# Top-k attention and gated FFN on one core: TensorE's order stated from step 14, six weight splits inside it, an even pace for the first FFN unit, and another row order in odd batches

## The chip, the cores and the metric

The kernel runs on one core of one Trainium2 chip. The metric is the device time of one execution in microseconds (us). Before the change three runs gave 1627.73, 1629.19 and 1631.22 us, median 1629.19. The core has five engines that run side by side and meet through semaphores: TensorE (PE; its weight load is listed apart as PEld), VectorE (DVE), ScalarE (ACT), GpSimd (POOL) and SyncE (SP). In this kernel SP issues every DMA, from one queue in program order.

## The reference

Eight batches of eight heads, 576 rows, head dimension 64. Each row of the scores keeps its 32 largest entries; the result of the attention, 4608 x 512, goes through a gated FFN:

```
scores = scale * np.matmul(q, k.transpose(0, 1, 3, 2))
kth = np.partition(scores, -top_k, axis=-1)[..., -top_k:-top_k + 1]      # top_k = 32
scores = np.where(scores >= kth, scores, -1000000000.0)
scores = scores - np.max(scores, axis=-1, keepdims=True)
attn = np.exp(scores)
attn = attn / (np.sum(attn, axis=-1, keepdims=True) + 1e-09)
x = np.matmul(attn, v)            # then 4608 rows x 512
gate = 1.0 / (1.0 + np.exp(-(x @ w_gate)))      # 512 x 1536
val = x @ w_val                                 # 512 x 1536
return gate * val @ w_out                       # 1536 x 512
```

The weights are handed over as 64-bit floats.

## The kernel before

**Attention.** Heads go in pairs (NP = 4 pairs). A batch's 576 rows are four tiles of 128 rows (i = 0 to 3) and a tile of the 64 remaining rows (i = 4). One step is one tile of one pair: 20 steps a batch, 160 in all. A batch is worked in two groups of tiles (`halves`, line 58), and a group goes through all four pairs before the next begins. In loop turn n, `begin(n+2)` multiplies the scores of step n+2 (`pss`), `choose(n)` starts the selection of step n (DVE's MAX8 rows, ACT's exponentials, POOL's products `u`) and ends that of step n-1, `turned(n-2)` transposes (`pt`), and `weighed` multiplies a group's attention with the values (`po`). Its result `xf` is split into a leading part `xh` (ACT, L371) and a rest `xl` (POOL, L372), both fp32r.

**FFN.** The 4608 rows go in 12 units of U = 384 rows. A unit is a generator of 432 matmuls; it is pulled forward piece by piece by `more(goal)`, between the attention's own chunks. Each product is three matmuls, of leading and rest parts (L404 to L406 for the two first products, L428 to L430 for the last). A unit uses 18 weight tiles of 1 MB: 12 for gate and value (indices 0 to 11) and 6 for the output (12 to 17), in the order 0 1 2 3, 12 13 with 4 drawn ahead of them from unit one on, 5 6 7, 14 15, 8 to 11, 16 17.

**Weights.** `split_weight` (L124) turns a 64-bit weight tile into a leading and a rest part, in two halves: a load of raw bits (`wraw`, L136), ACT L143, L147, L151, DVE L144 to L146, POOL L149 (two multiplies), PE L152 to L154 into a PSUM tile `wrest`, ACT L155, and a store to a DRAM tile `ws` (L156). The first 12 are split in steps 0 to 11. The six last (8 to 11, 16, 17) are split by the first FFN unit's own `load` (L381 to L387), which keeps the split tile in SBUF and uses it there. Every other `load` fetches the tile from `ws` (L389). All of these tiles, split or loaded, come from one pool `w` of three buffers, in turn; a tile can be filled only when the buffer's former tile has had its last reader, and a split tile that isn't kept is read last by its store to `ws`.

**What sets the order.** SP, DVE, ACT and POOL run what a scheduler arranged, in a fixed order per engine. PE's order is the scheduler's, too, until the splits are over (`split_done`, L158, called at L539 after unit 0 has been run to its end); from there it is the order in which the program states it (`tc.manual_schedule`, L566). `goal` (L577) says how far the FFN should be: `at` counts the rows that attention has finished, the FFN follows 480 rows behind (`BEHIND`), but unit 0, once its 384 rows are there, at 1.5 times attention's pace:

```
goal = max(at - BEHIND, min((at - U) * 1.5, U)) * per_row
```

An engine runs its instructions in order: while one waits, all behind it wait as well. This holds for SP's DMAs.

Of the kernel before, what the change touches and what calls it, by code (L numbers as in the profile page):

```python
# [29 lines left out]
def tile_topk_attention_then_gated_ffn(  # L30
# [27 lines left out]
    halves = {0: ((0, 3), (3, NT + 1)), 1: ((0, 2), (2, NT + 1))}  # L58
    groups = [(b, *half) for b in range(B) for half in halves[b % 2]]
# [3 lines left out]
    BEHIND = 480  # L63

    LOADED, HELD = 12, 0
# [50 lines left out]
    ready, stored = {}, set()  # L116
# [7 lines left out]
    def split_weight(idx, held):  # L124

        wt = pools["w"].tile([P, 2, 2, NP, P], F32R, tag="w", name=f"wsplit_{idx}")  # L130
        if held:
            ready[idx] = wt
        for i in range(2):
            raw = pre_pools["raw"].tile([P, NP * P, 2], U32, tag="raw", name=f"wraw_{idx}_{i}")
            half = slice(i * NP * P, (i + 1) * NP * P)
            nc.sync.dma_start(raw.rearrange("p n t -> p (n t)"), w[idx][:, half].bitcast(U32))  # L136
            low, top = raw[:, :, 0], raw[:, :, 1]
            pair = wt[:, i].rearrange("p a c n -> p a (c n)")
            lead = pre_pools["parts"].tile([P, NP * P], F32, tag="lead", name=f"wt_lead_{idx}_{i}")
            rest = ps_f.tile([P, NP * P], F32, tag="f", name=f"wrest_{idx}_{i}")  # L140
# [234 lines left out]
    def ffn(nm0, xs, t0, general, early):  # L375
# [87 lines left out]
    def run(general):  # L463
        steps = [(g, p, i) for g, (_, first, end) in enumerate(groups) for p in range(NP) for i in range(first, end)]
# [3 lines left out]
        def fetch_keys(m):  # L468
            if m < len(steps) and steps[m][2] == groups[steps[m][0]][1]:
                g, p, _ = steps[m]  # L470
                b, first, _ = groups[g]
                if first == 0:
                    keys[b, p] = load_keys(b, p, f"{mark}{g}_{p}")

        def fetch_values(m):
            if m < len(steps) and steps[m][2] == groups[steps[m][0]][1]:
# [29 lines left out]

        def more(upto):
# [8 lines left out]
        def turned(m):  # L516
            g, p, i = steps[m]
            b, first, end = groups[g]
            if i == first:
# [3 lines left out]
            ets[g, p].append((et, P if i < NT else REM))  # L523
            yield from turn(e, inv, i, et, f"{mark}{b}_{i}_{p}")

        def weighed(m):
            nonlocal unit
            g, p, i = steps[m]
            b, first, end = groups[g]
            if i < end - 1 or (g, p) not in ets:  # L530
                return
            t, left, pieces = b * S + first * P, sum(n for _, n in ets[g, p]), []
# [12 lines left out]
            if p == NP - 1:  # L545
                while (unit + 1) * U <= b * S + min(end * P, S):
                    todo.append(ffn(f"{mark}{unit}", [xs[unit, d] for d in range(NP)], unit * U, general, unit > 0))
# [13 lines left out]
        per_row = 3 * (2 * NF * NP + NE * NF)  # L561
        region = None

        for n in range(len(steps) + 3):
            if not general and region is None and len(bxs) == 2:
# [3 lines left out]
            if region is None and not general and n < len(steps) and steps[n][0] == 0:  # L569
                early, steps0 = LOADED + HELD, 3 * NP  # L570
                for t in range(n * early // steps0, (n + 1) * early // steps0):
                    split_weight(order[t], t >= LOADED)
                    stored.add(order[t])
            fetch_values(n)
            fetch_keys(n + KEYS)
            ask(n + ASK)
            goal = max(at - BEHIND, min((at - U) * 1.5, U)) * per_row  # L577
# [10 lines left out]
            else:  # L588
# [9 lines left out]
                for chunk in (first, second):  # L598
                    for _ in chunk:
                        pass  # L600
            if 2 <= n < len(steps) + 2:
                at += (P if steps[n - 2][2] < NT else REM) / NP
# [74 lines left out]
```

## Time and profile before

| | us |
|---|---|
| runs: lowest, median, highest | 1627.73, 1629.19, 1631.22 |
| the profiled execution's own time | 1630.14 |
| its span in the trace | 1628.3 |
| PE busy in the span | 1546.7 (95%) |
| PEld, DVE | 1420.9 (87%), 1247.9 (77%) |
| ACT, POOL | 1166.1 (72%), 1176.5 (72%) |
| first FFN matmul starts | 180.02 |
| last FFN unit | 1546.4 to 1621.4 |

The span is the time from the trace's first to its last instruction; 1.8 us of the execution lie outside it. A busy time is the sum over an engine's instructions. "Idle before" is the time for which an engine stood still ahead of an instruction, put down to the releaser that came last. PEclk is the granted TensorE clock, as a share of 2.4 GHz. A row of a view of stretches ("windows") gives for each engine the busy time in the stretch and, after x, the number of instructions.

### The profile page before, as it was taken

What the parts mean: (1) busy time and instruction counts of PE and PEld (TensorE: products, weight loads), DVE (VectorE), ACT (ScalarE), POOL (GpSimd) and SP (SyncE); (2) the same over time, 40 slices, a digit from 0 to 9 for tenths busy, and PEclk for the clock granted to TensorE, in tenths of its full rate; (3) what the DMA queues carried; (4) which work ended last, traced back from release to release, by engine and by line L of the source; (5) the groups of instructions that cost most, each with busy time, mean ns of one, the idle gap of its engine ahead of it and who ended that gap; (6) DMA issues with size and microseconds to landing.
All of it is one profiled execution on the core that took longest, in us unless ns stands there. A gap on an engine that the chain in (4) does not pass through costs nothing.

```text
span 1628.3 us, 35823 instructions
## 1 busy us (share of the span) xinstructions
PE 1546.7 (95%) x11378; PEld 1420.9 (87%) x11378; DVE 1247.9 (77%) x5764; ACT 1166.1 (72%) x2551; POOL 1176.5 (72%) x1907
## 2 busy tenths in 40 slices
PE   5787999989999999999999999999999999999998
PEld 2344797779999999999999999999999999999998
DVE  5999768968888779878889679788888679877100
ACT  5988658967867678777768678777778678767322
POOL 3869858887876887787876887787786887765323
PEclk9989899999999999999999999999999999999999
DMA  7556754655555665565555665565555665564475
GB/s 221 179 174 193 283 202 142 218 183 200 201 199 190 222 217 193 195 240 185 216 187 197 214 233 188 201 221 204 194 204 180 212 223 195 185 214 157 175 286 183
DMA packets 89000, 330.05 MB, mean 203 GB/s; under 512 B 9952, under 2 KB 36576, under 8 KB 61920
## 3 DMA queue, kind: packets, MB, share of 16 engines
q1 hardware_dynamic: 88800, 327.65, 58.0%
q8 instruction: 92, 1.51, 0.4%
q14 instruction: 108, 0.88, 0.2%
HBM read 299.30 MB, written 28.31 MB: 201 GB/s over the span
## 4 chain that ended last, share of the span: by engine, by line
PE 68%; DVE 10%; POOL 5%; ACT 5%; issue 2%; DMA 1%; POOLq 0%; ACTq 0%; DVEq 0%
PE pz L404 11%; PE pz L405 10%; PE pz L406 10%; PE pss L225 8%; PE po L364 7%; PE pt L328 5%; PE po L428 5%; PE po L429 5%; PE po L430 5%; DVE cand L291 3%; DVE e L245 2%; DVE kths L317 2%; POOL u L309 2%; ACT under L303 1%; POOL k L177 1%
## 5 line engine op out<-in xcount | busy, mean ns | idle before, releaser
L309 POOL TENSOR_TENSOR u<-s,under 128x288 f32<-128x288 f32 x576 | 412.2, 738 | 71.7 <-ACT under L303 59.8
L404 PE MATMUL pz<-xh,w 128*128 128x384 f32 x1120 | 405.5, 362 | 2.0 <-ACT xh L371 2.0
L291 DVE MAX8 cand<-s 128x8 f32<-128x72 f32 x2304 | 343.5, 217 | 68.7 <-ACT s L233 56.0
L405 PE MATMUL pz<-xl,w 128*128 128x384 f32 x1120 | 378.0, 338 | 3.6 <-POOL xl L372 3.6
L406 PE MATMUL pz<-xh,w 128*128 128x384 f32 x1120 | 378.4, 338 | 0.0
L245 DVE SCALAR_TENSOR_TENSOR e<-s,kths,e 128x576 f32<-128x576 f32 x288 | 280.8, 986 | 30.7 <-ACT e L240 29.8
L303 ACT ACTIVATE under<-s,leads 128x576 fp8e4<-128x576 f32 x288 | 222.5, 774 | 91.3 <-DVE leads L295 75.3
L317 DVE MAX8 kths<-u 128x8 f32<-128x584 f32 x288 | 219.1, 761 | 63.1 <-POOL u L310 60.8
L240 ACT ACTIVATE e<-s,st 128x576 f32<-128x576 f32 x288 | 209.9, 773 | 43.3 <-PE pt L328 36.6
L416 POOL TENSOR_TENSOR gl<-gf,gh 128x384 fp32r<-128x384 f32 x144 | 153.6, 1067 | 107.3 <-ACT gh L415 104.6
L404 PEld LDWEIGHTS pz<-xh,w 128*128 128x128 f32 x1120 | 212.1, 189 | 8.7 <-issue 4.6
L405 PEld LDWEIGHTS pz<-xl,w 128*128 128x128 f32 x1120 | 212.7, 190 | 5.3 <-POOL xl L372 4.8
L334 ACT ACTIVATE et<-pt 128x384 f32<-128x384 f32 (+1 forms) x384 | 194.9, 521 | 28.4 <-PE pt L328 24.5
L406 PEld LDWEIGHTS pz<-xh,w 128*128 128x128 f32 x1120 | 211.5, 189 | 0.0
L328 PE MATMUL pt<-ident,e 128*128 128x128 f32 x1152 | 193.1, 277 | 11.0 <-DVE e L245 5.5
L428 PE MATMUL po<-gh,w 128*128 128x384 f32 x560 | 201.1, 360 | 0.0
L429 PE MATMUL po<-gl,w 128*128 128x384 f32 x560 | 188.9, 337 | 5.2 <-POOL gl L416 5.2
L430 PE MATMUL po<-gh,w 128*128 128x384 f32 x560 | 188.4, 336 | 0.0
L364 PEld LDWEIGHTS po<-et,v 128*64 128x64 f32 x1600 | 160.2, 138 | 30.6 <-issue 20.7
L328 PEld LDWEIGHTS pt<-ident,e 128*128 128x128 f32 x1152 | 147.9, 142 | 40.8 <-issue 8.3
L364 PE MATMUL po<-et,v 128*64 128x128 f32 (+1 forms) x1600 | 180.2, 267 | 1.9 <-DVE xf L368 1.6
L365 PE MATMUL po<-et,v 128*64 128x128 f32 (+1 forms) x1600 | 180.4, 266 | 0.0
(97 smaller groups left out, 3340.5 us busy)
## 6 DMA issues: line engine op xcount, KB each, us to landing
w<-ws SPq DMA_DIRECT2D x210, 1024.0 KB, 4.9
v<-in_v_dram SPq DMA_DIRECT2D x64, 320.0 KB, 3.3
wraw<-in_w_dram SPq DMA_DIRECT2D x36, 512.0 KB, 4.1
ws<-wsplit SPq DMA_DIRECT2D x36, 512.0 KB, 3.5
qraw<-in_q_dram SPq DMA_DIRECT2D x140, 128.0 KB, 3.0
kraw<-in_k_dram SPq DMA_DIRECT2D x56, 288.0 KB, 4.1
out_dram<-acc SPq DMA_DIRECT2D x48, 192.0 KB, 4.9
q<-in_q_dram SPq DMA_DIRECT2D x20, 128.0 KB, 2.9
```

The source lines that it names most:

```text
L245: nc.vector.scalar_tensor_tensor(e[:, j], s[:, j], kth[j], e[:, j], op0=ALU.is_ge, op1=ALU.mult, accum_out=st[:, 4 + j : 5 + j])
L291: nc.vector.max(cand[:, j, 8 * g : 8 * g + 8], s[:, j, g * SEG : (g + 1) * SEG])
L309: nc.gpsimd.tensor_tensor(u[:, j, c], s[:, j, c], under[:, j, c], op=ALU.mult)
L317: nc.vector.max(kths[:, at[j] : at[j] + 8], u[:, j])
L328: nc.tensor.transpose(pt[:, c], ef[:, k0 : k0 + P], ident)
L364: nc.tensor.matmul(po[D:, c], vt[:, 5 + a], et[:, 4 + a, :n], start=a == 0, stop=a == 4)
L404: nc.tensor.matmul(ps, wt[:, u, 0, d], xh, start=d == 0, stop=False)
L405: nc.tensor.matmul(ps, wt[:, u, 0, d], xl, start=False, stop=False)
L406: nc.tensor.matmul(ps, wt[:, u, 1, d], xh, start=False, stop=d == NP - 1)
L428: nc.tensor.matmul(ps, wts[e // 2][:, e % 2, 0, f], gh, start=f == 0, stop=False)
L429: nc.tensor.matmul(ps, wts[e // 2][:, e % 2, 0, f], gl, start=False, stop=False)
L430: nc.tensor.matmul(ps, wts[e // 2][:, e % 2, 1, f], gh, start=False, stop=f == FG - 1)
```

## The change

Four things are changed.

1. **PE's order is stated from loop turn n = 14** (3*NP + 2), before the FFN has begun, instead of from the end of unit 0. What PE runs from there stands as the program writes it, chunk by chunk.
2. **The six last weights are split by the loop**, one in every two steps from n = 14: `split_weight` at the start of a step, and its PE matmuls, now in `split_rest` (L160 to L162), at the end of the following step, then ACT's copy and the store. The FFN's `load` fetches all 18 from `ws`, in unit 0 as well: six more loads of 1 MB.
3. **The pace**: `BEHIND` is 416 and the term of 1.5 times is gone. Unit 0 follows attention at attention's own pace like the others, and draws its weight 4 ahead (`early`) like the others. Where unit 0 was run to its end at once, `more(U * per_row)` runs what is left of it.
4. **Odd batches** do the tiles (0, 4) and then (1, 2, 3), so the 64 remaining rows come second; before they did (0, 1) and then (2, 3, 4). The host orders q and `row()` the result's rows to match.

```diff
-    halves = {0: ((0, 3), (3, NT + 1)), 1: ((0, 2), (2, NT + 1))}
-    groups = [(b, *half) for b in range(B) for half in halves[b % 2]]
+    halves = {0: ((0, 1, 2), (3, NT)), 1: ((0, NT), (1, 2, 3))}
+    groups = [(b, half) for b in range(B) for half in halves[b % 2]]
+
+    def row(b, i):
+        return b * S + (i * P + REM * (i > 0) if b % 2 and i < NT else P if b % 2 else i * P)
-    BEHIND = 480
-    LOADED, HELD = 12, 0
+    BEHIND = 416
+    LOADED = 12
...
-    def split_weight(idx, held):
+    def split_weight(idx):
         wt = pools["w"].tile([P, 2, 2, NP, P], F32R, tag="w", name=f"wsplit_{idx}")
-        if held:
-            ready[idx] = wt
+        halves = []
...
             nc.scalar.activation(pair[:, 0], bits, AF.Copy)
-            nc.tensor.matmul(rest, ident, bits, start=True, stop=False)
-            nc.tensor.matmul(rest, minus, pair[:, 0], start=False, stop=False)
-            nc.tensor.matmul(rest, plus, frac, start=False, stop=True)
+            halves.append((i, pair, bits))
+            if not stated:
+                split_rest(idx, *halves.pop())
+        return halves
+
+    def split_rest(idx, i, pair, bits):
+        frac = pair[:, 1]
+        rest = ps_f.tile([P, NP * P], F32, tag="f", name=f"wrest_{idx}_{i}")
+        nc.tensor.matmul(rest, ident, bits, start=True, stop=False)
+        nc.tensor.matmul(rest, minus, pair[:, 0], start=False, stop=False)
+        nc.tensor.matmul(rest, plus, frac, start=False, stop=True)
+        with urgent():
             nc.scalar.activation(pair[:, 1], rest, AF.Copy)
-            nc.sync.dma_start(w_split[idx][:, i], pair.bitcast(F32))
+        nc.sync.dma_start(w_split[idx][:, i], pair.bitcast(F32))
...
         def load(idx):
-            if idx in ready:
-                return ready.pop(idx)
-            if not (general or idx in stored):
-                split_weight(idx, True)
-                stored.add(idx)
-                return ready.pop(idx)
+            assert idx in stored
             wt = pools["w"].tile([P, 2, 2, NP, P], F32R, tag="w", name=f"w_{nm0}_{idx}")
             nc.sync.dma_start(wt.rearrange("p i a c n -> p i a (c n)").bitcast(F32), w_split[idx])
             return wt
...
                     if u % 3 == 2 and len(bxs) == 1:
-                        for _ in todo.pop(0) if todo else ():
-                            pass
+                        more(U * per_row)
                         split_done()
...
-            if not general and region is None and len(bxs) == 2:
+            if not general and n == 3 * NP + 2:
                 region = tc.manual_schedule(engines={mybir.EngineType.PE})
...
+            if region is not None and len(stored) < n_w and not halves:
+                idx = order[len(stored)]
+                halves = split_weight(idx)
+                fresh = True
+            else:
+                fresh = False
...
-            goal = max(at - BEHIND, min((at - U) * 1.5, U)) * per_row
+            goal = max(at - BEHIND, 0) * per_row
...
                 for chunk in (first, second):
                     for _ in chunk:
                         pass
+                if halves and not fresh:
+                    for half in halves:
+                        split_rest(idx, *half)
+                    stored.add(idx)
+                    halves = []
```

How this moves instructions shows at three places. Numbers behind a name are the batch, tile and pair of an attention tile (`pss_0_3_3_0`: batch 0, tile 3, pair 3), the weight and half of a split (`wrest_15_1`), and unit and weight of a loaded tile (`w_0_5`); the last number of a name is a counter.

First, PE where the FFN's first matmul (`pz_0_0_0_0`) stands. Before:

```order
L364 MATMUL po_0_4_0_2072<-et_0_4_0_2056,v_1_0_1668 64x64
L365 MATMUL po_0_4_0_2072<-et_0_4_0_2056,v_1_0_1668 64x64
L328 MATMUL pt_0_3_1_1_2220<-ident_105,e_0_3_1_1868 128x128 x3
L152 MATMUL wrest_15_1_1576<-wraw_15_1_1573,ident_105 128x512
L404 MATMUL pz_0_0_0_0_1979<-xh_0_0_739,w_0_0_1974 128x384
L405 MATMUL pz_0_0_0_0_1979<-xl_0_0_740,w_0_0_1974 128x384
```

And now:

```order
L160 MATMUL wrest_15_1_1584<-wraw_15_1_1573,ident_105 128x512
L161 MATMUL wrest_15_1_1584<-wsplit_15_1555,minus_163 128x512
L160 MATMUL wrest_8_0_2013<-wraw_8_0_1854,ident_105 128x512
L161 MATMUL wrest_8_0_2013<-wsplit_8_1853,minus_163 128x512
L162 MATMUL wrest_15_1_1584<-wsplit_15_1555,plus_162 128x512
L162 MATMUL wrest_8_0_2013<-wsplit_8_1853,plus_162 128x512
L160 MATMUL wrest_8_1_2019<-wraw_8_1_1865,ident_105 128x512
L161 MATMUL wrest_8_1_2019<-wsplit_8_1853,minus_163 128x512
L162 MATMUL wrest_8_1_2019<-wsplit_8_1853,plus_162 128x512
L217 MATMUL pss_0_3_3_0_2118<-k_0_3_6_815,q_0_3_3_1878 128x288 x2
L408 MATMUL pz_0_0_0_0_2127<-xh_0_0_739,w_0_0_2122 128x384
L409 MATMUL pz_0_0_0_0_2127<-xl_0_0_740,w_0_0_2122 128x384
```

The rest of weight 15 and the whole of weight 8's PE part now stand ahead of the FFN's first matmul: eight rows more. 26 rows of attention that stood ahead of it before (20 of `po_0_4_0`, six of `pt_0_3_1`) now stand behind it.

Second, PE in unit 0 where weight 5 is first used. Before, behind weight 4, which was loaded one buffer earlier:

```order
L404 MATMUL pz_0_1_0_1_2506<-xh_0_3_1810,w_0_4_2487 128x384
L405 MATMUL pz_0_1_0_1_2506<-xl_0_3_1811,w_0_4_2487 128x384
L406 MATMUL pz_0_1_0_1_2506<-xh_0_3_1810,w_0_4_2487 128x384
L404 MATMUL pz_0_1_1_0_2597<-xh_0_0_739,w_0_5_2592 128x384
L405 MATMUL pz_0_1_1_0_2597<-xl_0_0_740,w_0_5_2592 128x384
```

And now, behind weight 13, whose buffer weight 5 takes over:

```order
L337 MATMUL pt_1_0_0_0_3037<-ident_105,e_1_0_0_2680 128x128 x3
L432 MATMUL po2_0_0_3_2915<-gh_0_0_3_2555,w_0_13_2898 128x384
L433 MATMUL po2_0_0_3_2915<-gl_0_0_3_2556,w_0_13_2898 128x384
L434 MATMUL po2_0_0_3_2915<-gh_0_0_3_2555,w_0_13_2898 128x384
L337 MATMUL pt_1_0_0_1_3047<-ident_105,e_1_0_0_2680 128x128 x3
L408 MATMUL pz_0_1_1_0_3057<-xh_0_0_739,w_0_5_3052 128x384
L409 MATMUL pz_0_1_1_0_3057<-xl_0_0_740,w_0_5_3052 128x384
```

Three transposes are all that stands between the last matmul on weight 13 and the first on weight 5. The other two of the three buffers hold the split tiles 11 and 16 at that point.

Third, SP's queue in unit 0, where the loads of weights 5 to 8 stand. Before, loads stand one behind the other:

```order
L389 DMA w_0_5_2592<-ws5_128 128x2048 [waits DMAHW4_49,PE_49]
L183 DMA v_2_0_2704<-in_v_dram 128x640 [waits PE_49]
L389 DMA w_0_6_2627<-ws6_129 128x2048 [waits DMAHW6_49,PE_49]
L192 DMA qraw_1_1_3_3239<-in_q_dram 128x256 [waits DMAHW5_49,Pool_49]
L389 DMA w_0_7_2786<-ws7_130 128x2048 [waits DMAHW1_49,PE_49]
```

And now:

```order
L393 DMA w_0_5_3052<-ws5_128 128x2048 [waits DMAHW1_49,DMAHW0_49,PE_49]
L393 DMA w_0_6_3194<-ws6_129 128x2048 [waits DMAHW7_49,DMAHW5_49]
L201 DMA qraw_1_1_1_3673<-in_q_dram 128x256 [waits DMAHW2_49,Pool_49]
L192 DMA v_2_2_3264<-in_v_dram 128x640 [waits DMAHW3_49,PE_49]
L201 DMA qraw_1_2_1_3795<-in_q_dram 128x256 [waits DMAHW4_49,Pool_49]
L137 DMA wraw_17_0_3242<-in_w_dram 128x1024 [waits PE_49]
L165 DMA ws16_139<-wsplit_16_2934 128x1024 [waits DMAHW6_49,Activation_49]
L137 DMA wraw_17_1_3253<-in_w_dram 128x1024 [waits DVE_49,PE_49]
L165 DMA ws16_139<-wsplit_16_2934 128x1024 [waits DMAHW0_49,Activation_49]
L393 DMA w_0_7_3328<-ws7_130 128x2048 [waits DMAHW1_49]
L393 DMA w_0_8_3473<-ws8_131 128x2048 [waits DMAHW2_49,DMAHW6_49,DMAHW0_49,PE_49]
```

The raw loads and stores of the splits have come between the loads of the FFN, and weight 7's load stands behind both stores of weight 16, which wait for ACT.

## Rows read from the trace of the kernel before

**Rows 1.** The page: busy time, share of the span, instructions of each engine
```profile
PE 1546.7 (95%) x11378; PEld 1420.9 (87%) x11378; DVE 1247.9 (77%) x5764; ACT 1166.1 (72%) x2551; POOL 1176.5 (72%) x1907
```

**Rows 2.** The page: the chain that ended last, share of the span
```profile
PE 68%; DVE 10%; POOL 5%; ACT 5%; issue 2%; DMA 1%; POOLq 0%; ACTq 0%; DVEq 0%
```

**Rows 3.** Stretches: us; PE, PEld, DVE, ACT, POOL busy (x); PEclk; DMA share; GB/s
```profile
180.00:260.00 80.00, 80.00 (x523) 71.29 (x522) 54.47 (x241) 49.30 (x111) 55.61 (x89) 0.98 0.55 198
260.00:364.00 104.00, 92.93 (x599) 78.16 (x598) 88.36 (x374) 85.66 (x184) 87.11 (x132) 0.95 0.59 200
313.00:317.00 4.00, 3.27 (x11) 3.27 (x12) 4.00 (x15) 2.79 (x9) 3.23 (x5) 0.57 0.83 341
344.00:351.00 7.00, 6.47 (x19) 6.07 (x20) 2.74 (x18) 3.98 (x11) 6.81 (x14) 0.51 0.18 53
364.00:728.00 364.00, 359.44 (x2808) 346.17 (x2807) 299.31 (x1418) 273.73 (x611) 285.30 (x469) 1.00 0.59 206
```

**Rows 4.** PE's waits: line and releaser: total us, times, longest us
```profile
PE pz L405 <- POOL xl L372: 3.6, 4, 1.2
...
PE pz L404 <- ACT xh L371: 2.0, 1, 2.0
```

**Rows 5.** PE's timeline at the FFN's start: start us, us, instruction [idle before]
```profile
179.44 1.40 PE L152 MATMUL wrest<-wraw,ident 128*128 128x512 f32 x2 [2.04 <-DVE wraw L145]
180.02 1.13 PE L404 MATMUL pz<-xh,w 128*128 128x384 f32 x1
```

**Rows 6.** POOL's timeline: weight 15's second half, and what follows it
```profile
184.38 1.88 POOL L149 TENSOR_TENSOR wsplit<-wsplit,wt_lead 128x256 fp32r<-128x256 f32 x2
...
187.53 2.08 POOL L309 TENSOR_TENSOR u<-s,under 128x288 f32<-128x288 f32 x2
```

**Rows 7.** ACT's timeline: the same half's copy
```profile
189.81 0.60 ACT L155 ACTIVATE wsplit<-wrest 128x512 fp32r<-128x512 f32 x1
```

**Rows 8.** SP's timeline: its store, and a weight load ahead of it
```profile
186.72 0.33 SPq L389 DMA_DIRECT2D w<-ws  x1
...
191.16 0.38 SPq L156 DMA_DIRECT2D ws<-wsplit  x1
```

**Rows 9.** The page, DMA issues: count, KB each, median us to landing
```profile
w<-ws SPq DMA_DIRECT2D x210, 1024.0 KB, 4.9
...
wraw<-in_w_dram SPq DMA_DIRECT2D x36, 512.0 KB, 4.1
ws<-wsplit SPq DMA_DIRECT2D x36, 512.0 KB, 3.5
```

**Rows 10.** The tile w: its loads
```profile
DMA to landing us min/median/max: 4.6/4.9/8.0
```

**Rows 11.** Groups by line: the splits' matmuls and POOL's multiply, busy, mean ns
```profile
L152 PE MATMUL wrest<-wraw,ident 128*128 128x512 f32 x72 | 48.1, 754 | 9.2 <-DVE wraw L145 8.8 <-ACT s L233 0.3
L153 PE MATMUL wrest<-wsplit,minus 128*128 128x512 f32 x36 | 20.5, 570 | 2.5 <-ACT wsplit L151 2.5
L154 PE MATMUL wrest<-wsplit,plus 128*128 128x512 f32 x36 | 17.7, 491 | 8.2 <-POOL wsplit L149 8.2
...
L149 POOL TENSOR_TENSOR wsplit<-wsplit,wt_lead 128x256 fp32r<-128x256 f32 x72 | 61.0, 868 | 20.7 <-DVE cand L291 13.1 <-DVE wt_lead L146 3.0 <-DVE tops L295 2.8
```

**Rows 12.** PE's timeline: 40 weighing matmuls, first and last, and unit one's start
```profile
337.84 0.32 PE L364 MATMUL po<-et,v 128*64 128x128 f32 x1 [1.61 <-DVE xf L368]
...
339.97 0.27 PE L365 MATMUL po<-et,v 128*64 128x128 f32 x1
...
344.02 0.68 PE L404 MATMUL pz<-xh,w 128*128 128x384 f32 x1 [2.01 <-ACT xh L371]
```

**Rows 13.** PE's timeline at unit four's start, with three transposes
```profile
713.81 0.44 PE L405 MATMUL pz<-xl,w 128*128 128x384 f32 x1 [1.23 <-POOL xl L372]
...
714.27 0.49 PE L328 MATMUL pt<-ident,e 128*128 128x128 f32 x3
```

More of the change, by code (lines that the diff above doesn't have):

```diff
@@ L56, in tile_topk_attention_then_gated_ffn, with size @@
     U = 3 * P
-    halves = {0: ((0, 3), (3, NT + 1)), 1: ((0, 2), (2, NT + 1))}
-    groups = [(b, *half) for b in range(B) for half in halves[b % 2]]
+    halves = {0: ((0, 1, 2), (3, NT)), 1: ((0, NT), (1, 2, 3))}
+    groups = [(b, half) for b in range(B) for half in halves[b % 2]]
+    def size(i):
+        return P if i < NT else REM
+    def row(b, i):
+        return b * S + (i * P + REM * (i > 0) if b % 2 and i < NT else P if b % 2 else i * P)
     KEYS, ASK, AHEAD = 4, 4, 2
-    BEHIND = 480
-    LOADED, HELD = 12, 0
+    BEHIND = 416
+    LOADED = 12
     WHOLE = 1
@@ L463, in run @@
     def run(general):
-        steps = [(g, p, i) for g, (_, first, end) in enumerate(groups) for p in range(NP) for i in range(first, end)]
+        steps = [(g, p, i) for g, (_, tiles) in enumerate(groups) for p in range(NP) for i in tiles]
         keys, values, qs, staged, xs = {}, {}, {}, {}, {}
@@ L468, in fetch_keys @@
         def fetch_keys(m):
-            if m < len(steps) and steps[m][2] == groups[steps[m][0]][1]:
+            if m < len(steps) and steps[m][2] == groups[steps[m][0]][1][0]:
                 g, p, _ = steps[m]
-                b, first, _ = groups[g]
-                if first == 0:
+                b, tiles = groups[g]
+                if tiles[0] == 0:
                     keys[b, p] = load_keys(b, p, f"{mark}{g}_{p}")
         def fetch_values(m):
-            if m < len(steps) and steps[m][2] == groups[steps[m][0]][1]:
+            if m < len(steps) and steps[m][2] == groups[steps[m][0]][1][0]:
                 g, p, _ = steps[m]
@@ L517, in turned @@
             g, p, i = steps[m]
-            b, first, end = groups[g]
-            if i == first:
+            b, tiles = groups[g]
+            if i == tiles[0]:
                 ets[g, p] = []
@@ L522, in turned @@
             e, inv = done.pop(m)
-            ets[g, p].append((et, P if i < NT else REM))
+            ets[g, p].append((et, size(i)))
             yield from turn(e, inv, i, et, f"{mark}{b}_{i}_{p}")
@@ L528, in weighed @@
             g, p, i = steps[m]
-            b, first, end = groups[g]
-            if i < end - 1 or (g, p) not in ets:
+            b, tiles = groups[g]
+            if i != tiles[-1] or (g, p) not in ets:
                 return
-            t, left, pieces = b * S + first * P, sum(n for _, n in ets[g, p]), []
+            t, left, pieces = row(b, tiles[0]), sum(n for _, n in ets[g, p]), []
             while left:
@@ L545, in weighed @@
             if p == NP - 1:
-                while (unit + 1) * U <= b * S + min(end * P, S):
-                    todo.append(ffn(f"{mark}{unit}", [xs[unit, d] for d in range(NP)], unit * U, general, unit > 0))
+                while (unit + 1) * U <= t:
+                    todo.append(ffn(f"{mark}{unit}", [xs[unit, d] for d in range(NP)], unit * U, not general))
                     unit += 1
@@ L568, in run @@
                 stated.append(region)
[L569 to L572, printed above, removed]
+            if not general and n < 3 * NP:
+                for t in range(n * LOADED // (3 * NP), (n + 1) * LOADED // (3 * NP)):
+                    split_weight(order[t])
                     stored.add(order[t])
+            if region is not None and len(stored) < n_w and not halves:
[4 more added lines that the diff above has]
+                fresh = False
             fetch_values(n)
@@ L600, in run @@
                         pass
+                if halves and not fresh:
[3 more added lines that the diff above has]
+                    halves = []
             if 2 <= n < len(steps) + 2:
-                at += (P if steps[n - 2][2] < NT else REM) / NP
+                at += size(steps[n - 2][2]) / NP
         for rest in todo:
@@ L642 @@
     kt = np.concatenate([kt, kt], axis=2)
-    qt = np.swapaxes(q, 2, 3).reshape(B, H // 2, 2, D, S)
+    qt = np.swapaxes(q, 2, 3).reshape(B, H // 2, 2, D, S).copy()
+    qt[1::2] = np.concatenate([qt[1::2, ..., :P], qt[1::2, ..., P + R :], qt[1::2, ..., P : P + R]], axis=-1)
     ql = np.zeros((B, NT + 1, H // 2, D, 2, P), q.dtype)
```

9 lines of the change are left out of this document (4 added, 5 removed).

## The prediction

> **What bounds the kernel now.** I read the page first: PE is busy for 95% of the span, DVE for 77%, ACT and POOL for 72% [rows 1], and PE holds 68% of the chain that ended last, DVE 10% [rows 2]. So PE sets the time nearly everywhere, and a change is worth what it takes from PE's idle and half-clock time, or adds to it. Then the stretches, to see where PE is idle [rows 3]. From 364 on it is busy 359.44 of 364 us, idle 4.6, or 1.3 in 104. From 180 to 260, with unit 0 at 1.5 times the pace, it is busy for all 80 us, while DVE, ACT and POOL have 49 to 56 us of work. From 260 to 364, where the five last weights are split and unit 0 runs out, it is busy only 92.93 of 104 us, and DVE, ACT and POOL are at 82 to 85%. The granted clock shows in the same view: 0.57 of 2.4 GHz in 313 to 317 and 0.51 in 344 to 351, the lower level, 1.2 GHz. The second follows waits at the start of unit one. PE's list of waits has no wait for a weight load, which is why no row of one stands here; what it has at the starts of units is small [rows 4].
>
> The change acts between 165 and about 380 us. PE's and SP's orders are the same as before for the first 268 PE rows, up to about 165 us. So I add up what it does to PE's idle time from there on, against the execution's own time of 1630.14 us.
>
> **A. The FFN begins later: +14 us (7 to 20).** Before, the first FFN matmul starts at 180.02 us [rows 5]. Now the splits of weights 15 and 8 stand ahead of it in PE's stated order, and weight 0's tile takes the buffer of split tile 15, so its load waits until both stores of weight 15 have landed. The path, with before's times: POOL ends the second half of weight 15 at 184.38 + 1.88 = 186.26, and it is not free sooner, because long products stand ahead of it in both orders [rows 6]; ACT's copy ends at 189.81 + 0.60 = 190.41 [rows 7]; the store is issued at 191.16 [rows 8]; it lands after 3.5, the load after another 4.9 [rows 9]: 199.6. From below: if PE, free of FFN work, takes the half up when POOL ends it, one matmul of 0.49 [rows 11], a copy of 0.60, 3.5 and 4.9 give 195.8. I take 198, 18 us later. Weight 8's POOL products don't come later than that: they follow one product `u` of 2.08 us [rows 6] with 4 x 0.868 us [rows 11]. Not all of the 18 us is lost. Eight split rows are done meanwhile that came later before: at most 2 halves x (1.40 + 0.57 + 0.49) for weight 8 and 0.57 + 0.49 for weight 15, 6.0 us [rows 5, 11]; 26 attention rows go the other way, 20 weighing rows at 2.13 us per 40 rows and 6 transposes at 0.49 per 3, about 2.1 us [rows 12, 13]. Net 3.9 us done: 18 - 3.9 = 14. Bounds: 195.8 with all 6.0 us kept gives about 10, and 7 if weight 15's half also comes 3 us earlier; a start at 202, where weight 8's raw load (4.1 us [rows 9]) comes late, gives 20 with 1.7 us kept. Attention is held up as well, since its transposes stand behind the FFN's first matmul on PE.
>
> **B. The even pace: -12 us (-15 to -4).** What before loses in 260 to 364 is 11.07 us idle less the usual 1.3, 9.8; and the half clock costs 4.00 x 0.43 + 7.00 x 0.49 = 5.1 [rows 3]. All of it is 14.9. An even pace leaves FFN matmuls between the attention's chunks to fill these gaps. I take 12 and not 14.9, because six splits go on while DVE, ACT and POOL are close to what they were in 260 to 364, where 82 to 85% of busy time went with gaps on PE. From above: if the splits make these gaps whatever the FFN's pace, only the half clock and little else comes back, 4 us.
>
> **C. Weight loads that PE waits for: +15 us (8 to 22).** This is the part that I weigh most. Before, no split was in flight while unit 0 loaded its first twelve tiles, so all three buffers of `w` took turns, and a load had the time of a whole tile's matmuls to land in. Now a split tile holds a buffer for two steps and until its stores have landed. At four places the order leaves a load nothing to hide behind; a load is 4.9 us at the median and 4.6 at the least [rows 10], plus 0.33 for its issue [rows 8].
> - Weight 12 takes the buffer of weight 4, which is used directly before it; between them stand only 20 weighing rows, some 1 to 1.8 us: a wait of 5.2 - 1.8 = 3.4.
> - Weight 5 takes the buffer of weight 13; between them stand three transposes, 0.49 [rows 13]: 4.7.
> - Weight 7 stands on SP behind both stores of weight 16, which wait for ACT's copy after the last PE row of that split. Copy 0.6, two issues 0.7, landing 4.9, less four score matmuls of about 0.5: 5.7.
> - Weight 3 waits for weight 9's stores to land: 3.5 + 4.9 from a store that is issued about 7 us ahead: 1.4.
> Together 15.2. What stands behind these matmuls on PE, the transposes and scores, waits as well, so neither ACT nor DVE can use the time. From below: weight 3 and 7 hidden and the loads at their least, 3.1 + 4.4 = 7.5, 8. From above: each of three other loads (1, 2, 14) adds some 2 us: 22.
>
> **D. Half clock behind such waits: +3 us (0 to 8).** After waits of 1.61, 2.01 and less at unit one's start [rows 12], 7 us ran at 0.51, a loss of 3.4 [rows 3]. Before unit 0's first matmul there is now a longer wait, and three of C's are longer, too. One such stretch is 3.4 us; I take 3 in all, because steady stretches at 1.00 hold waits of 1.2 us without one.
>
> **E. Starts of units: -3 us (-4 to +3).** PE waits 3.6 us in four places for POOL's `xl`, the first rows of units 4, 7 and 10 among them [rows 4], up to 1.23 each [rows 13]. With 416 rows behind and 64 rows second in odd batches, 61 to 69 PE rows of other work stand between a weigh and the unit that reads it, where there were none. The upper bound is what a new gap of the same size would cost at three other starts.
>
> **F. At nothing.** Six more loads of 1 MB: DMA is busy at 0.55 to 0.59 [rows 3], and each load that PE does wait for is in C. The FFN ends 416 instead of 480 rows behind attention: the same matmuls move from the tail to before it, on an engine that is full in both.
>
> **The sum**: 14 - 12 + 15 + 3 - 3 = +17 us. 1630.14 + 17 = 1647.1; the median of the three runs lies 0.95 below the profiled execution, so 1646 is what I predict. Taking the terms' bounds as independent, the likeliest case by itself reaches from 1635 to 1661.
>
> One rule of the Trainium skill bears on C: "Perfetto Trace Analysis", section "Optimization Strategy", says that the same gap repeating on the engine that should be saturated can mean that there is not enough SBUF for the next tile. No run here shows such gaps yet; by the rule they would come with the splits in the pool and end with them, which is what C says from the buffers' order.
>
> **Rivals.**
>
> *The pace pays and the loads are hidden* (18%). If the scheduler's other engines run ahead far enough (ACT, DVE and POOL get 18 us of rest before the FFN starts), splits end earlier than I think, their buffers come free, and C and D vanish. Then 8 - 15 - 3 = -10 us, about 1619. For it: PE stood idle 11 us in 260 to 364, and gaps on PE are all that this kernel can win. Against it: at weight 5 and weight 12 the load's buffer is read on PE itself until a few rows before, and no earlier split changes that. The same section of "Perfetto Trace Analysis" says that interleaving stretches with different bounds may improve performance; the trace agrees that there are two, 180 to 260 with PE full and 260 to 364 with the others near it, and by that rule alone the time would be this rival's.
>
> *The terms cancel* (10%). With A, C and D near their lower ends and B at its upper one, 7 - 15 + 8 + 2 - 3 = -1: within 3.3 us of before.
>
> *Slower still* (10%). The splits' PSUM tiles share three buffers with the FFN's sums, and PE's order is fixed: a `wrest` that stands ahead of a sum waits until DVE has read the last one, and DVE's turn stands behind the long products of a later attention step. Its price is one such wait at each of the 12 halves, up to 2 us each as `wrest` shows in waits for DVE and POOL (8.8 and 8.2 us in six and seven waits [rows 11]): +15 to +24, 1661 to 1670. It decides if DVE is over some 90% busy in 200 to 330.
>
> **How the numbers follow.** The forecast, slower by 6 to 32 us, has 62%. The range that should hold 8 in 10 is 1622 to 1661: it takes in the cancelling case and part of the fast one, and leaves out some 12% below and 8% above. What a measurement of this kernel can tell from no change is 0.2%, 3.3 us. Faster by more: 18%; within it: 10%; slower by more: 62 + 10 = 72%.
>
> **What would show it.** The first `pz` of unit 0 at 196 to 200 us (A). In PE's list of waits, `pz` and `po` waiting for DMA `w<-ws`, 8 to 22 us in four to seven waits, the longest near 5 (C). PE's idle time from 200 to the start of unit one mostly these (B), the lower clock right behind them (D). No wait for `xl` at the starts of units 4, 7 and 10 (E), and from 400 us on stretches of 364 us that read like those before. I am wrong if no wait for `w<-ws` over 2 us is there, or if the FFN starts before 190.

## The result and the profile after

The changed kernel took 1650.12 us (median of four runs, 1649.08 to 1652.41), the kernel before 1630.20 in runs beside it: a ratio of 1.0123, 95% interval 1.0101 to 1.0145. It is slower by 19.9 us, where 17 were forecast. The profiled execution took 1652.41 us, with a span of 1650.6.

Busy times from the page, to be read against [rows 1]:

```profile
PE 1549.5 (94%) x11378; PEld 1429.4 (87%) x11378; DVE 1253.4 (76%) x5764; ACT 1166.6 (71%) x2535; POOL 1170.1 (71%) x1891
```

PE does the same work (1549.5 against 1546.7 us) in a longer span. So the loss is time in which PE stood still or ran slowly. Stretches of the changed kernel, in the columns of [rows 3]:

```profile
180.00:200.00 20.00, 12.09 (x27) 6.38 (x27) 13.61 (x31) 8.54 (x15) 15.66 (x24) 0.50 0.74 249
200.00:260.00 60.00, 49.88 (x349) 43.93 (x348) 39.87 (x165) 40.44 (x87) 39.37 (x62) 0.90 0.63 216
260.00:364.00 104.00, 85.62 (x603) 78.39 (x602) 66.49 (x298) 67.89 (x148) 57.19 (x96) 0.92 0.56 193
364.00:728.00 364.00, 361.91 (x2859) 349.67 (x2859) 299.97 (x1418) 272.69 (x605) 281.38 (x461) 1.00 0.60 208
```

From 364 us on PE is busier than before (361.91 against 359.44 of 364). All of the loss lies between 165 and 364: from 180 to 200 only 27 matmuls run, at the lower clock, and from 200 to 364 PE is idle 28.5 us, while DVE, ACT and POOL are at 55 to 65% in the last 104 us. In [rows 3] they were at 82 to 85% there. So it is not these engines that PE waits for.

What it waits for, in the list of PE's waits from 200 to 364 us (line and releaser: total us, times, longest):

```profile
PE pz L408 <- DMA w<-ws: 22.8, 3, 9.7
PE po L432 <- DMA w<-ws: 5.5, 1, 5.5
```

Four waits for weight loads, 28.3 us in all; the one other wait in the list is of 0.2 us. PE's timeline, cut to the rows with these waits and the FFN's first matmul, the counterpart of [rows 5]:

```profile
196.79 0.69 PE L408 MATMUL pz<-xh,w 128*128 128x384 f32 x1 [0.36 <-DMA w<-ws]
...
231.82 0.47 PE L408 MATMUL pz<-xh,w 128*128 128x384 f32 x1 [4.64 <-DMA w<-ws]
...
254.54 0.69 PE L432 MATMUL po<-gh,w 128*128 128x384 f32 x1 [5.47 <-DMA w<-ws]
...
280.21 0.66 PE L408 MATMUL pz<-xh,w 128*128 128x384 f32 x1 [8.44 <-DMA w<-ws]
...
308.15 0.66 PE L408 MATMUL pz<-xh,w 128*128 128x384 f32 x1 [9.70 <-DMA w<-ws]
```

By the stated order these are the first matmuls on weights 0, 3, 12, 5 and 7. The last four are the places that the prediction named, and each wait there is longer than it said. The clock right behind them, in stretches of 2 us (PE busy, PEclk, DMA share, GB/s):

```profile
232.00:234.00 2.00, 2.00 (x8) 0.52 0.95 400
254.00:256.00 2.00, 1.46 (x5) 0.50 0.97 393
280.00:282.00 2.00, 1.79 (x6) 0.50 0.54 221
308.00:310.00 2.00, 1.85 (x7) 0.50 0.83 336
```

Behind every one of the four PE runs at the lower level, 1.2 GHz. The other two columns are the first hint of what stretched the loads. The same columns for each of the four loads, from its issue to PE's first matmul on it (the issues follow below):

```profile
226.60:231.80 5.20, 0.58 (x6) 1.00 0.90 318
247.30:254.50 7.20, 1.76 (x40) 0.87 1.00 357
271.50:280.20 8.70, 0.28 (x3) 0.79 0.96 343
299.30:308.10 8.80, 0.00 (x0) 0.75 0.98 344
```

While these loads are on the way, the 16 DMA engines are busy for 0.90 to 1.00 of the time and move 318 to 357 GB/s; from 364 to 728 us it is 0.60 and 208. The splits' transfers come in bursts that fill the DMA engines, and the shares of the long stretches above, 0.56 and 0.63, hide that.

SP's timeline around the load of weight 5 (start, duration, line, transfer):

```profile
267.75 0.33 SPq L137 DMA_DIRECT2D wraw<-in_w_dram  x1
268.84 0.33 SPq L165 DMA_DIRECT2D ws<-wsplit  x1
269.25 0.38 SPq L137 DMA_DIRECT2D wraw<-in_w_dram  x1
270.20 0.47 SPq L165 DMA_DIRECT2D ws<-wsplit  x1
271.48 5.79 SPq L393 DMA_DIRECT2D w<-ws  x2
```

Two raw loads and two stores, 2 MB, are issued in the 3.7 us ahead of the load; it is issued at 271.5 and PE can start at 280.2, 8.7 us later instead of the usual 4.9. Read in the same way, the other three are issued at 226.60 (weight 3), 247.27 (12) and 299.31 (7) and let PE start 5.2, 7.3 and 8.8 us later. What the four places share is here: the load stands behind both stores of a split, and these wait for matmuls that PE has done a moment ago. Whether the buffer (as I had it) or the neighbours in the queue hold the load is what the experiments had to tell.

### The profile page after: what moved, and what is told of

Same layout as the page of the kernel before. It is cut to its first block, busy times and chain, and to the rows that moved or that the text cites. A ratio compares the mean times of both kernels' runs of the same rounds, so it can differ in the third digit from the quotient of the medians.

```text
span 1650.6 us, 35748 instructions
## 1 busy us (share of the span) xinstructions
PE 1549.5 (94%) x11378; PEld 1429.4 (87%) x11378; DVE 1253.4 (76%) x5764; ACT 1166.6 (71%) x2535; POOL 1170.1 (71%) x1891
## 4 chain that ended last, share of the span: by engine, by line
PE 64%; DVE 7%; POOL 7%; ACT 4%; DMA 4%; issue 2%; POOLq 0%; SPq 0%; ACTq 0%
PE pz L408 10%; PE pz L410 9%; PE pz L409 9%; PE pss L234 7%; PE po L373 7%; PE po L432 5%; PE pt L337 5%; PE po L434 5%; PE po L433 5%; POOL u L318 3%; DMA w<-ws 3%; DVE cand L300 2%; DVE kths L326 2%; DVE e L254 1%; POOL k L186 1%
## 5 line engine op out<-in xcount | busy, mean ns | idle before, releaser
L318 POOL TENSOR_TENSOR u<-s,under 128x288 f32<-128x288 f32 x576 | 420.4, 753 | 89.0 <-ACT under L312 81.9
L408 PE MATMUL pz<-xh,w 128*128 128x384 f32 x1152 | 419.0, 364 | 23.1 <-DMA w<-ws 23.1
L410 PE MATMUL pz<-xh,w 128*128 128x384 f32 x1152 | 389.7, 338 | 0.0
L409 PE MATMUL pz<-xl,w 128*128 128x384 f32 x1152 | 388.8, 337 | 0.0
L254 DVE SCALAR_TENSOR_TENSOR e<-s,kths,e 128x576 f32<-128x576 f32 x288 | 276.8, 965 | 49.5 <-ACT e L249 49.0
L408 PEld LDWEIGHTS pz<-xh,w 128*128 128x128 f32 x1152 | 218.4, 190 | 28.9 <-issue 21.3
L409 PEld LDWEIGHTS pz<-xl,w 128*128 128x128 f32 x1152 | 219.1, 190 | 0.0
L432 PE MATMUL po<-gh,w 128*128 128x384 f32 x576 | 209.8, 364 | 9.9 <-DMA w<-ws 5.5
L410 PEld LDWEIGHTS pz<-xh,w 128*128 128x128 f32 x1152 | 217.9, 189 | 0.0
L420 POOL TENSOR_TENSOR gl<-gf,gh 128x384 fp32r<-128x384 f32 x144 | 149.7, 1040 | 92.4 <-ACT gh L419 89.4
L434 PE MATMUL po<-gh,w 128*128 128x384 f32 x576 | 194.3, 337 | 0.0
L433 PE MATMUL po<-gl,w 128*128 128x384 f32 x576 | 193.7, 336 | 0.0
```

What stands on the lines that cost most here:

```text
L254: nc.vector.scalar_tensor_tensor(e[:, j], s[:, j], kth[j], e[:, j], op0=ALU.is_ge, op1=ALU.mult, accum_out=st[:, 4 + j : 5 + j])
L318: nc.gpsimd.tensor_tensor(u[:, j, c], s[:, j, c], under[:, j, c], op=ALU.mult)
L408: nc.tensor.matmul(ps, wt[:, u, 0, d], xh, start=d == 0, stop=False)
L409: nc.tensor.matmul(ps, wt[:, u, 0, d], xl, start=False, stop=False)
L410: nc.tensor.matmul(ps, wt[:, u, 1, d], xh, start=False, stop=d == NP - 1)
L432: nc.tensor.matmul(ps, wts[e // 2][:, e % 2, 0, f], gh, start=f == 0, stop=False)
```

## The experiments

Times are medians of runs beside the kernel before, whose median was 1628.1 to 1630.9 us in the three sets. The ratio is to that median, with its 95% interval. The first set asked whether the splits in flight cause the waits, and by what.

**All 18 weights split in the first 12 steps.**

```diff
-    LOADED = 12
+    LOADED = 18
```

> Theory 1: PE waits for weight loads in unit 0 because split tiles hold the buffers of the pool and because the splits' raw loads and stores stand in front of the loads. With all 18 weights split in the first 12 steps (order of PE still stated from step 14, unit 0 still loads all 18, the same pace) no split is in flight after about 200 us: no wait for a weight load above 1 us from 205 on, so the changed kernel's 28 us of such waits and some 3 us of half clock go; the six splits cost up to 10 us more ahead of the FFN. About 1622 us (1615 to 1632). Theory 2: the stated order itself, or the six more loads, makes the waits: they stay at 20 us or more and the time is 1645 to 1665.

Measured: 1641.43 us, ratio 1.0084 (1.0064 to 1.0105), between the times of the two theories. No wait for a weight load is left in PE's list from 165 to 364 us; that half of theory 1 holds, and theory 2 falls: the same stated order and the same six more loads wait for nothing once no split is between them. But the six splits cost far more than 10 us ahead of the FFN, which now begins at 234 us. From 165 to 364 the list reads:

```profile
PE wrest L160 <- DVE wraw L145: 18.0, 11, 2.9
PE wrest L162 <- POOL wsplit L149: 4.9, 4, 3.5
PE wrest L161 <- ACT wsplit L151: 2.2, 2, 1.8
...
```

PE waits for the split's other engines instead. None of them is full: from 165 to 234 us DVE, ACT and POOL are busy for 58 to 62% of the time, and PE for 63%, at a granted clock of 0.64. What holds the splits there was not followed up.

**Later splits, 14 of them early.** The edit of the run above with 14 in place of 12, and the others only from step 17 on:

```diff
-            if region is not None and len(stored) < n_w and not halves:
+            if n >= 17 and region is not None and len(stored) < n_w and not halves:
```

> 14 weights are split in the first 12 steps and the other four from step 17 on, one per two steps. Theory 1: the FFN's first tile is drawn from the pool directly behind the last early split and no PE row of a later split stands ahead of the FFN, so the FFN starts at 180 to 190 us and not at 197; but four splits are in flight while unit 0 loads, so waits for weight loads stay at 10 to 25 us. About 1636 us (1628 to 1645). Theory 2 (the late start has nothing to do with the splits stated ahead of it): the FFN starts at 197 or later, and the time is 1645 or more.

Measured: 1656.52 us, 1.0184 (1.0159 to 1.0209), and the FFN begins at 204.8 us: a miss, with both figures where theory 2 put them. The run mixes two things, two more splits in the crowded first stage and a later start of the rest, so it doesn't settle the start; waits for loads are 25.2 us. The later run with twelve does it cleanly.

**Four weight buffers**, and its control with three; both with smaller pools elsewhere to make room:

```diff
-    bqr = ctx.enter_context(tc.tile_pool(name="bqr", bufs=3))
+    bqr = ctx.enter_context(tc.tile_pool(name="bqr", bufs=2))
...
-    for name, bufs in (("w", 3), ("f2", 3), ("f4", NE + 1), ("fg", FG + 2)):
+    for name, bufs in (("w", 4), ("f2", 3), ("f4", NE), ("fg", FG + 1)):
```

> The changed kernel with four buffers in the weight pool, and room made by one buffer less of the accumulators, of the two gate pools and of the raw queries. Theory 1 (buffers): waits for weight loads fall from 28 us to under 8, also because a load that is issued a tile ahead doesn't mind the transfers in front of it; the FFN's first load no longer waits for weight 15's stores. 1615 to 1630 us if the control with three buffers and the same small pools is near 1650. Theory 2 (the DMA queue, not the buffers, sets the landing): waits stay at 15 us or more, and the time is within 8 us of the control.

> Control for the run with four buffers: the changed kernel with the same smaller pools and three weight buffers. Both theories: 1648 to 1662 us; what the smaller pools cost by themselves is 0 to 10 us, and the waits for weight loads are those of the changed kernel, 25 to 30 us.

Measured: 1649.87 us with four buffers (1.0123, 1.0096 to 1.0149), 1651.27 with three (1.0140, 1.0120 to 1.0160). A fourth buffer is worth nothing that can be measured; the control waits 27.5 us for loads. PE's waits with four, from 165 to 364:

```profile
PE pz L408 <- DMA w<-ws: 20.9, 3, 10.1
...
PE po L432 <- DMA w<-ws: 5.4, 1, 5.4
```

The same four waits. In this kernel's order on SP, none of the four loads waits for PE any more, only for an earlier transfer; the one of weight 5:

```
L165 DMA ws11_134<-wsplit_11_2633 128x1024 [waits DMAHW6_49,Activation_49]
L393 DMA w_0_5_3052<-ws5_128 128x2048 [waits DMAHW7_49]
```

So the buffers are free, and each load is issued the moment the second store lets it through. SP's timeline, cut to these four places:

```profile
220.59 0.83 SPq L165 DMA_DIRECT2D ws<-wsplit  x1
221.47 0.90 SPq L393 DMA_DIRECT2D w<-ws  x1
...
241.96 0.63 SPq L165 DMA_DIRECT2D ws<-wsplit  x1
242.64 2.83 SPq L393 DMA_DIRECT2D w<-ws  x2
...
267.81 0.47 SPq L165 DMA_DIRECT2D ws<-wsplit  x1
268.34 2.14 SPq L393 DMA_DIRECT2D w<-ws  x2
...
295.87 0.59 SPq L165 DMA_DIRECT2D ws<-wsplit  x1
296.51 6.85 SPq L393 DMA_DIRECT2D w<-ws  x3
```

And PE's, cut to the first matmuls that wait for them:

```profile
231.24 0.46 PE L408 MATMUL pz<-xh,w 128*128 128x384 f32 x1 [2.82 <-DMA w<-ws]
...
252.33 0.69 PE L432 MATMUL po<-gh,w 128*128 128x384 f32 x1 [5.40 <-DMA w<-ws]
...
277.38 0.66 PE L408 MATMUL pz<-xh,w 128*128 128x384 f32 x1 [7.99 <-DMA w<-ws]
...
305.80 0.66 PE L408 MATMUL pz<-xh,w 128*128 128x384 f32 x1 [10.07 <-DMA w<-ws]
```

From issue to matmul they now take 9.8, 9.7, 9.0 and 9.3 us, twice the usual 4.9, and all that time the DMA engines are at 0.97 to 1.01. Weights 3 and 12 are issued 5 us sooner than in the changed kernel and reach PE only 0.6 and 2.2 us sooner: they are on the way beside two raw loads and two stores. So the buffers are a lock, but not the one that decides; my theory of them falls as the sufficient cause. What is left is the place: behind the stores in SP's order, and among their transfers. The second set was made for that.

**Weights asked for a tile ahead**, three buffers. When the program first uses a unit's weight tile it asks for the next one, so that the load stands earlier in SP's order:

```diff
         def load(idx):
-            assert idx in stored
-            wt = pools["w"].tile([P, 2, 2, NP, P], F32R, tag="w", name=f"w_{nm0}_{idx}")
-            nc.sync.dma_start(wt.rearrange("p i a c n -> p i a (c n)").bitcast(F32), w_split[idx])
+            wt = fetched.pop(idx) if idx in fetched else fetch(idx)
+            nxt = ahead_of.get(idx)
+            if early and nxt in stored:
+                fetched[nxt] = fetch(nxt)
             return wt
```

> Four buffers changed nothing: the loads of weights 3, 12, 5 and 7 had their buffer free and still stood on SP behind the stores of the split whose last matmuls PE had just done. Theory 3 (place in SP's queue): with the program asking for a unit's next weight tile when the present one is first used, three buffers, all else as in the changed kernel, the loads stand ahead of those stores; waits for weight loads fall from 28 us to under 8, and the time to about 1624 us (1617 to 1632). Rival (buffers, or the bandwidth that the splits' transfers take): waits stay above 15 us and the time above 1638.

Measured: 1628.09 us, 1.0002 (0.9990 to 1.0015): 22 us less than the changed kernel, back at the time of before. The FFN still begins at 196.4 us, so none of the 22 is its start. PE's waits from 165 to 364 (L424 is the line that was L408):

```profile
PE wrest L160 <- DVE wraw L145: 7.2, 3, 3.7
PE wrest L162 <- POOL wsplit L149: 4.8, 2, 4.0
PE pz L424 <- DMA w<-ws: 4.6, 3, 2.9
PE wrest L161 <- ACT wsplit L151: 4.1, 1, 4.1
...
```

Waits for loads fall from 28.3 us from 200 on (28.6 with the 0.4 at the FFN's start) to 4.6, and the landing of a weight load from 196 to 345 us is back at a median of 4.9, where the changed kernel had 5.6 and a maximum of 8.7:

```profile
DMA to landing us min/median/max: 4.7/4.9/6.9
```

The edit moves the loads' place in the queue and the turn of the buffers at once: weight 12 now takes the buffer of weight 3, not 4, and weight 5 that of weight 12, not 13. Free buffers alone change nothing, as the run with four shows.

**The later splits, with twelve early.** The condition of the second run with `n >= 18`, and `LOADED` at 12:

> Twelve weights split early as in the changed kernel; the six others from step 18 on, one per two steps, so that none of their PE rows stands ahead of the FFN's first matmul and the FFN's first load follows weight 14's buffer. Theory on the start (term A): FFN starts at 178 to 186 us instead of 197, 10 to 14 us come back; the waits for weight loads stay at 20 to 30 us, as loads still stand behind stores. About 1637 us (1631 to 1644). Rival: the early phase sets the start and it stays at 193 or later: 1647 to 1653.

Measured: 1651.43 us, 1.0130 (1.0109 to 1.0151). The start came back, the time did not: the FFN begins at 184.6 us, 12 sooner, and the waits for loads grow to 34 us, five of them over 3 us where the changed kernel had four:

```profile
PE pz L408 <- DMA w<-ws: 24.1, 4, 9.7
PE po L432 <- DMA w<-ws: 9.9, 2, 6.0
```

What the start gains, the waits for loads and the slower clock behind them take back (PEclk 0.86 from 260 to 364, against 0.92): the splits now meet unit 0's loads at other places, and one more of them is caught.

**Both edits.**

> Both edits. If theory 3 and the one on the start hold they add up: 1650 - 12 - 26 = 1612 us (1603 to 1622), faster than the kernel before. If the two are the same loss seen twice: 1624 to 1636.

Measured: 1619.28 us, 0.9940 (0.9919 to 0.9961), 9 us less than before and faster than both kernels. The FFN's start, against [rows 5]:

```profile
178.75 2.08 PE L160 MATMUL wrest<-wraw,ident 128*128 128x512 f32 x2 [6.25 <-DVE wraw L145]
179.84 1.31 PE L424 MATMUL pz<-xh,w 128*128 128x384 f32 x1
```

It stands where before had it, 180 us, and the waits for loads from there to 364 are 3.4 us. With the queue open, the later splits and the earlier start that they give are worth 8.8 us (1628.09 to 1619.28); with the queue in the way they were worth nothing. The sum is 7 us short of the forecast of this run, 26 for the queue being 22 and 12 for the start being 9.

**The stores on ACT's queue**, three buffers, loads not asked for ahead:

```diff
-        nc.sync.dma_start(w_split[idx][:, i], pair.bitcast(F32))
+        (nc.scalar if stated else nc.sync).dma_start(w_split[idx][:, i], pair.bitcast(F32))
```

> The changed kernel with the splits' stores from step 14 on issued by ACT, right behind ACT's copy, so that no load on SP stands behind a store; the raw loads, which wait for PE and DVE, stay on SP ahead of the loads, and three buffers stay. Theory 3 in its narrow form (the stores alone): waits fall to under 12 us, 1630 to 1636. Theory 3 with raw loads and buffers as second locks behind the first: waits stay at 20 to 28 us, 1643 to 1651.

Measured: 1651.89 us, 1.0142 (1.0121 to 1.0163), waits for loads 26.9 us:

```profile
PE pz L408 <- DMA w<-ws: 20.8, 5, 8.9
...
PE po L432 <- DMA w<-ws: 6.1, 1, 6.1
```

The second reading holds. There are several locks on such a load: the stores on SP, the raw loads on SP (which wait for PE and DVE), the buffer, and the 2 MB that are on the way at the same time from whichever queue. Four buffers open one, ACT's queue another, and neither alone helps. Asking a tile ahead gives a load the time of a tile to get past them. How much of the 28.3 us is standing in SP's queue and how much is sharing full DMA engines stays open: no run changes one and leaves the other.

**Parts of the change on the kernel before.** The last set was to price the pace and the row order by themselves. Row order and 416 rows behind; the even pace; both. The edit of the pace:

```diff
-            goal = max(at - BEHIND, min((at - U) * 1.5, U)) * per_row
+            goal = max(at - BEHIND, 0) * per_row
```

> The kernel before with only the odd batches' new row order and 416 rows behind (terms E and F alone). From 364 us on the changed kernel's trace lost 5 us less on PE than before, and its list of waits has no xl. If the row order and 416 make that, this run takes 3 to 6 us less than before, about 1624. If the stated order or the drawing ahead of unit 0 makes it: within 2 us of before.

> The kernel before with only the pace of unit 0 changed: goal = max(at - 480, 0), no 1.5 times; splits still inside unit 0's own loads, PE's order there still the scheduler's (term B by itself). If the even pace is what fills PE's gaps of 260 to 364: 6 to 16 us less, 1613 to 1622. If it needs the splits out of unit 0's loads as well: within 4 us of before or slower, since the splits then come while less time is left for unit 0.

> The kernel before with row order, 416 rows behind and the even pace, without the stated order and the moved splits (terms B, E and F). If B is the pace alone: 1608 to 1618, and the moved splits with the stated order are what costs the rest. If not: 1622 to 1632.

Measured: 1986.88 (1.2192, 1.2162 to 1.2223), 1824.69 (1.1190, 1.1157 to 1.1222) and 1983.48 us (1.2168, 1.2133 to 1.2202). All three are misses, and by something else than they were to test. Stretches of the first of them:

```profile
400.00:450.00 50.00, 41.97 (x266) 37.75 (x264) 31.23 (x165) 34.13 (x72) 31.31 (x49) 0.83 0.51 175
450.00:500.00 50.00, 39.30 (x273) 35.09 (x274) 42.61 (x215) 31.80 (x71) 35.88 (x64) 0.82 0.23 78
500.00:550.00 50.00, 50.00 (x292) 49.97 (x291) 6.35 (x13) 13.89 (x27) 12.58 (x14) 1.00 0.69 251
```

FFN and attention no longer interleave but take turns: from 500 to 550 PE does FFN alone and DVE has 6.35 us of work; before that DVE works and PE has gaps. The reading is from the code: before runs unit 0 (the head of `todo`) to its end when the splits close, and does not count that in `work`. By its goal, 48 of 384 rows are left then, a small lead. With the even pace 256 are left, and with the new row order unit 0 is already gone and 352 of the 384 rows of unit 1 are run; the FFN is so far ahead of its count that it eats each unit at once and then waits for rows. The change's `more(U * per_row)` counts what it runs. That line belongs to the even pace and the row order, and I had left it behind in these three. The lead itself was not measured; the row order and the pace alone stay unpriced.

**Ten early splits**, the rest from step 15, loads asked for ahead:

> The faster kernel of the last call (weights asked for a tile ahead) with ten early splits instead of twelve and the other eight from step 15 on, one per two steps. If each early split costs the first stage some 2 us, as the run with 18 suggests: 1612 to 1618 us. If the eight then crowd unit 0 as before: 1619 to 1630.

Measured: 1652.64 us, 1.0141 (1.0111 to 1.0172). The FFN begins at 166.2 us, 30 sooner than in the changed kernel, and all of that is lost again: eight splits in unit 0 crowd it, as the second reading had it, though by more than it said. Its loads wait, from 165 to 400 us:

```profile
PE pz L424 <- DMA w<-ws: 17.9, 3, 6.9
...
PE po L448 <- DMA w<-ws: 5.3, 1, 5.3
```

PE waits for DVE (11.6 us) and POOL (2.6 us) beside that. The best version found is the one with twelve early splits, the rest from step 18, and loads asked for a tile ahead.

## Why the prediction was right, point by point

The direction and the size were right, 17 us forecast and 19.9 measured. To compare the terms I count each PE instruction of both traces at the median time to its successor in the steady part, and call the rest of a stretch lost. This is an estimate: other choices of the median move the two differences from 165 to 364 us by some 3 us. Before loses 5.6 us from 165 to 180 and 28.2 from there to 364; after loses 20.6 from 165 to 196.8 and 41.7 from there to 364; from 364 on 82.8 and 77.8. With 1.1 us more ahead of 165 and 2.4 less work, the differences make 22.2, which is about the difference of the spans, 22.3. (The profiled execution of the changed kernel is the slowest of its four runs, so this is more than the 19.9 of the medians.)

- **A, the late start: +14 forecast, +15.0 by this count.** The FFN begins at 196.8; 198 was forecast. Both causes named are in the trace: the last split rows stand ahead, and the load lands at nearly the same moment (a wait of 0.36). The runs with the later splits put it back to 184.6 and 179.8.
- **B and D, the even pace and the half clock: -9 together forecast, -15 by this count** (41.7 less 28.3 of load waits, against 28.2). PE's gaps of 260 to 364 us are gone: without the load waits only 0.2 us of waits stand in the list. I had allowed 3 us for gaps that the splits would leave, and that allowance was not needed. The half clock showed behind every one of the four long waits. B and D are not told apart by a run, and B alone was not measured. The granted clock gives an estimate of D: in stretches of 1 us, PE ran at 0.50 for some 3.4, 4.9, 3.1 and 5.9 us behind the four waits, 17.3 in all, of which half is lost, 8.7 against the 5.1 that the prediction read in before. That is +3.6 for D where 3 was forecast, and it leaves some -18 for B, which would be beyond its bound of -15.
- **C, the load waits: +15 forecast, 28.3 measured.** This is the term that was mis-sized, beyond its upper bound of 22. The places were right, all four; the waits were 4.6, 5.5, 8.4 and 9.7 where 1.4, 3.4, 4.7 and 5.7 were forecast. The step that failed is "a load is 4.9 us at the median and 4.6 at the least": most loads of that row are in steady stretches, and its maximum, 8.0, was left out of the sum. Here they took 5.2, 7.3, 8.7 and 8.8 us from issue to matmul, 10.4 more than four times 4.9, while the splits' transfers kept the DMA engines busy for 0.90 to 1.00 of the time; without that the four waits would be 17.9. The other 2.7 are mostly weight 3's, whose load was issued 7.3 us behind the second store (219.31 to 226.60), not the 3.5 I gave the store. The reason was too narrow as well: at weights 3, 12 and 5 the prediction blamed the buffer, and with the buffers free the waits were still 26.3 us. The prediction cited the Trainium skill, "Perfetto Trace Analysis", section "Optimization Strategy", that repeating gaps on the engine that should be full can mean too little SBUF for the next tile. The gaps came and went with the splits as it had it, but a fourth buffer left them: here the measurement says that a load's place and neighbours decide.
- **E, unit starts: -3 forecast, -5.0 from 364 on by the count.** The list of waits from 364 us on had 3.1 us for `xl` before and has none; `gl` (5.2 us) went too, and a wait for `part` (4.4) came. By the trace alone, not by a run.
- **F at nothing:** with all splits early, the six more loads of unit 0 land without a wait. The 416 rows were not priced by a run.

That the sum came out near is in part luck: C took 13 us more than I allowed, and by the count B gave some 6 more back. The rival "the pace pays and the loads are hidden" worked out 1619, and the two edits together measured 1619.28. That the figures meet is a coincidence: the rival kept 8 us for a late start and got there by splits that end earlier, while this run splits later, starts the FFN at 179.8 and asks for the loads earlier. Of the 31 us between it and the changed kernel, 22 came with the place of the loads and 9 with the later splits. The prediction's argument against that rival, that at weights 5 and 12 the buffer is read until a few rows before, missed that asking earlier also changes which buffer a load takes.

## What to carry to other kernels

Where one engine issues all DMAs, read its queue, not only its buffers: here four loads behind stores that waited for a fresh result cost PE 28.3 us of waits, and a fourth buffer did not help. State the load where it has time, a tile ahead, when the compute order is stated by hand. And take a load's price from a stretch with the same neighbours: the same 1 MB was 4.9 us in steady stretches and 8.7 behind 2 MB of others. A mean DMA share of 0.6 says little about that, since the share in the bursts was near 1.

## What was not expected of the hardware

The slower clock behind a long wait was term D; its size in the three failed runs was not expected. PE has gaps throughout there, and stretches of 50 us stand at 0.82 and 0.83 in the first of them. PE's busy time rose to 1707.0, 1626.5 and 1701.4 us for the same 11378 matmuls that take 1546.7 before. In these runs a gap on PE cost more than its length.
